# Attention, softplus-tanh layer and experts on one core: weight decoding one piece per step, softmax division moved to VectorE, loads interleaved with the attention steps

## The chip, the cores and the metric

One core of one Trainium2 chip runs the whole program. The time is device microseconds of one execution, and versions are compared by the median of several executions. Engine names below: PE is TensorE, ACT is ScalarE, DVE is VectorE, POOL is GpSimd, and SP is the engine whose queue issues all transfers here.

## What is computed

Three stages follow one another. The first is an attention with two branches for 2 batches, 8 heads, 576 positions and 64 dimensions: a global branch over averages of four positions, and a local branch in which each position sees only the positions less than four away. The second is a dense layer pair, the third eight experts with a balanced gate.

```python
q_d, k_d, v_d = (t.reshape(B, H, S // 4, 4, D).mean(axis=3) for t in (q, k, v))
out_up = np.repeat(sm_attn(q_d, k_d, v_d), 4, axis=2)            # global branch
mask = np.abs(pos[:, None] - pos[None, :]) < 4
scores = np.where(mask, scale * q @ k.T, -1e9)                   # local branch
attn = np.exp(scores - scores.max(-1)); attn = attn / (attn.sum(-1) + 1e-9)
x = (out_up + attn @ v)                                          # 1152 tokens x 512
h = x @ w_in                                                     # 512 -> 2048
g = h * np.tanh(softplus(h))
x = g @ w_out                                                    # 2048 -> 512
out = sum over 8 experts of P[:, e] * (relu(x @ w1[e]) @ w2[e])  # P: gate, balanced in 8 rounds
```

The drawn weights `w_in` and `w_out` arrive as 64-bit floating point numbers; the chip computes on 32-bit ones.

## The kernel before, in words

Products are made from pairs of a rounded part and a rest (`hi` and `lo`), three products for each, so that a 128x128 block of weights meets 288 tokens in three matrix products.

**The start** brings the first half of batch 0's attention alone (the first 54 us, in which the change moves nothing). **The slots** come behind it: the loop `for s in range(NS + LAG)` runs the dense pair as 64 slots. Slot `s` does `gemm1(s)` (12 products of `w_in` into a bank, L505), then `mish(s)` (the elementwise chain L485 to L493, over ACT, POOL and DVE, which ends in `ghi` on ACT and `glo`), and `gemm2(s - 4)` (12 products of `w_out`, L528). A token group has 288 tokens, three attention tiles of 96; slots 0 to 5 work on the first group, 6 to 11 on the second, 12 to 17 on the third.

**The waves** lie in the same slots: while slots 0 to 5 run, the attention of the next three tiles is made, and so on: three waves of six slots, each for half a batch. A wave's steps (`attn_steps`) are called one by one by `pump`, between the matrix products of the slots. A step is one part of a unit. A global unit (`gunit`) and a local unit (`lunit`) have three each: `sc` (scores on PE, maximum on DVE L301, exponentials on ACT L303, row sums and their reciprocals on DVE L305 and L306, multiplication by the reciprocals L308), `tr` (transposes on PE) and `av` (product with the values, sum of both branches L393, `xhi` on ACT L394, `xlo` on DVE L395). Each wave has two global and three local units. The first `gemm1` of the next slot group reads `xhi` and `xlo` of all three tiles. `prep` (L267, L280, L282) turns keys and queries before a wave's units; `prep_v` adds up the values on POOL.

**The decoding** turns the 64-bit weights into 32-bit ones. The 8 column blocks of `w_in` and 8 row blocks of `w_out` form a list of 16 (`ring`), each done as two halves by `w_raw`: one ACT copy (L180), three DVE operations on 128x512 (L181, L183, L184), then the request for the half that comes two halves later (`load_w64`, two buffers `raw64`, 512 KB each). `w_split` cuts a decoded block into `hi` (ACT L190) and `lo` (POOL L191). In each slot the loop calls `w_raw` up to twice: once if the next half is wanted within 16 slots, and again if it is wanted within 6. Blocks 0 and 1 are decoded in the start.

**Order.** Each engine executes its instructions in a fixed order. That order is set when the program is built, by a scheduler that places instructions by its own timeline and may move them ahead of earlier ones; `tc.issue_after(x)` keeps what follows it from being placed ahead of `x`. On the chip an instruction that waits holds up everything behind it on its engine.

**Transfers** of keys, queries and values of the second batch, and of the near rows' values for each tile (`load_vw`, 102 rows), go through SP's one queue. In the before version a wave's steps are: all `prep`, then (in the first wave) the second batch's keys and queries, then the values of three tiles, then the units.

**The experts** come behind slot 63; nothing there is changed.

Of the kernel before, what the change touches and what calls it, by code (L numbers as in the profile page):

```python
# [24 lines left out]
AHEAD = 16  # L25
VWB = 3
# [12 lines left out]
def attn_moe_moe_kernel(  # L39
# [13 lines left out]
    PE, ACT, DVE, POOL, SP = nc.tensor, nc.scalar, nc.vector, nc.gpsimd, nc.sync  # L53
    B, H, S, D = q.shape
# [27 lines left out]
    def f32(a):  # L82
        return a.bitcast(F32)

    def new(pool, shape, dt, tag, bufs=2):
        return pool.tile(shape, dt, tag=tag, name=tag, bufs=bufs)
# [27 lines left out]
    state = {"start": True, "n": 0, "g": 0, "pg": 0}  # L114
# [4 lines left out]
    def at_bank():  # L119
        state["n"] += 1  # L120
        return bank("acc" if state["start"] and state["n"] % 2 else "w")

    last = {}
# [10 lines left out]
    ATT_END = 2 * next(i for i, x in enumerate(items) if x[0] == 3)  # L134
# [12 lines left out]
    need = {(kind, m): 2 * loads[m][0] + LAG * (kind == 2) for m in range(len(order)) for kind in (1, 2)}  # L147
    ring = sorted(need, key=need.get)
    raw64, wraw, whl = {}, {}, {}
    place = {"load": 0, "raw": 0, "split": 0}  # L150
# [15 lines left out]
    def w_raw():  # L166

        n, i = divmod(place["raw"], 2)  # L170
        if n >= len(ring) or n >= place["split"] + RAWB:
            return
        place["raw"] += 1
        if i == 0:
            own = n % RAWB == ERAW
            wraw[n] = new(ap if own else wp, [128, 1024], F32, "rawx" if own else "raw", 1 if own else ERAW)
        w = raw64.pop((n, i)).rearrange("p (n t) -> p n t", t=2)
        c = slice(512 * i, 512 * i + 512)
        lo, hi, x = w[:, :, 0], w[:, :, 1], wraw[n].bitcast(U32)[:, c]
        ACT.activation(out=f32(x), in_=f32(hi), func=AF.Copy, scale=F64_BIAS)  # L180
        DVE.tensor_scalar(out=x, in0=x, scalar1=3, scalar2=0x7FFFFFF8, op0=ALU.logical_shift_left,  # L181
                          op1=ALU.bitwise_and)
        DVE.scalar_tensor_tensor(out=x, in0=hi, scalar=0x80000000, in1=x, op0=ALU.bitwise_and, op1=ALU.bitwise_or)  # L183
        DVE.scalar_tensor_tensor(out=x, in0=lo, scalar=29, in1=x, op0=ALU.logical_shift_right, op1=ALU.bitwise_or)  # L184
        load_w64()
# [109 lines left out]
    def softmax(s3, p, rows, tag):  # L295

        n, nh, nk = s3[0].shape
        den = new(at, [n, 2, nh], F32, tag + "d", 2)
        for par in range(2):
            nm = new(at, [n, nh], F32, tag + "m", 4)  # L300
            DVE.tensor_reduce(out=nm, in_=s3[par], axis=AX.X, op=ALU.max, negate=True)  # L301
            for i in range(nh):
                exps.append(ACT.activation(out=p[par][:, i], in_=s3[par][:, i], func=AF.Exp, bias=nm[:, i:i + 1],  # L303
                                           scale=1.0, accum_out=den[:, par, i:i + 1]))
        DVE.tensor_scalar(out=den, in0=den, scalar1=1e-9, scalar2=rows, op0=ALU.add, op1=ALU.mult)  # L305
        DVE.reciprocal(out=den, in_=den)  # L306
        for par in range(2):
            (DVE if par and state["start"] else POOL).tensor_tensor(  # L308
                out=p[par], in0=p[par], in1=den[:, par].unsqueeze(2).to_broadcast([n, nh, nk]), op=ALU.mult)

    def gunit(b, half, q4):


        u = {}
        hps = (2 * q4, 2 * q4 + 1)

        def sc():
            bks = [at_bank() for _ in range(2)]
            for i, hp in enumerate(hps):
                for par, bk in enumerate(bks):  # L320
                    o = slice(64 * par, 64 * par + 64)
                    PE.matmul(out=bk[:SH, SD * i:SD * i + SD], lhsT=qd[b, half][o, hp, :], rhs=kd[b][o, hp, :],
                              start=True, stop=True)
            for par in range(2):
                u[par] = pg[state["pg"] % PBG]
                state["pg"] += 1
            softmax([bk[:SH, 0:2 * SD].rearrange("p (a b) -> p a b", b=SD) for bk in bks], u, 4.0, "g")

        def tr():
            u["pt"] = new(at, [W, 8 * TQ], F32, "pt", 2)[:SH, 0:8 * SH].rearrange("p (a b) -> p a b", a=8)  # L330
            for par in range(2):
                bk = at_bank()
                for i in range(2):
                    for c in range(2):
                        j = 2 * i + c
                        PE.transpose(out=bk[:SH, SH * j:SH * j + SH], in_=u[par][:, i, SH * c:SH * c + SH],
                                     identity=ident[:SH, :SH])
                ACT.activation(out=u["pt"][:, 4 * par:4 * par + 4, :].rearrange("p a b -> p (a b)"),
                               in_=bk[:SH, 0:4 * SH], func=AF.Copy)

        def av():
            if (b, half) not in odT:
                odT[b, half] = new(at, [128, HP, SH], F32, "odT", 1)
            bk = at_bank()
            for i, hp in enumerate(hps):
                for c in range(2):
                    for par in range(2):
                        PE.matmul(out=bk[64 * par:64 * par + 64, SH * i:SH * i + SH], lhsT=vd[b, c][:, 2 * hp + par, :],
                                  rhs=u["pt"][:, 4 * par + 2 * i + c, :], start=(c == 0), stop=(c == 1))
            ACT.activation(out=odT[b, half][:, hps[0]:hps[0] + 2, :].rearrange("p a b -> p (a b)"),  # L350
                           in_=bk[:, 0:2 * SH], func=AF.Copy)
        return [sc, tr, av]
# [45 lines left out]
    def piped(units):  # L398

        return [units[i - 2 * s][s] for i in range(len(units) + 4) for s in (2, 1, 0) if 0 <= i - 2 * s < len(units)]  # L400

    def hb_steps(hb):

        b, half = divmod(hb, 2)
        st = []
        if half == 0:
            st += [partial(prep, "k", b, 0, hp) for hp in range(HP)]
            st += [partial(prep, "q", b, 0, hp) for hp in range(HP)]
            st += [partial(load4, "v", b, 0), partial(load4, "v", b, 1)]
            st += [partial(prep, "k", b, 1, hp) for hp in range(HP)]  # L410
            st += [partial(load4, "q", b, 1)]
            st += [partial(prep_v, b, 0), partial(prep_v, b, 1)]
        else:
            st += [partial(prep, "q", b, 1, hp) for hp in range(HP)]
            if b + 1 < B:
                st += [partial(load4, "k", b + 1, 0), partial(load4, "q", b + 1, 0), partial(load4, "k", b + 1, 1)]
        return st

    def attn_steps(t0, t1):
        st, units = [], []  # L420
        for t in range(t0, t1):
            if t % 3 == 0:
                st += piped(units) if units else []
                st += hb_steps(t // 3)
                units = [gunit(*divmod(t // 3, 2), i) for i in range(2)]
            if t >= VWB:
                st.append(partial(load_vw, t))
            units.append(lunit(t))
        return st + piped(units)


    groups = [(sum(TPG[:i]), n) for i, n in enumerate(TPG)]
# [159 lines left out]
    for s in range(NS + LAG):  # L592
        if s == NS - 4:
            with tc.issue_after(last["mish"].ins):
                gate()
        for a, b, st in waves:
            if s == b:
                while steps:
                    steps.pop(0)()
            if s == b == waves[-1][1]:  # L600
                at_ctx.close()
                tp = ctx.enter_context(tc.tile_pool(name="tp", bufs=1, side="right", reuse_waits="tile"))
                tx["hi"], tx["lo"] = (tp.tile([128, 3 * KH, NB], F32R, name=f"t{z}") for z in ("hi", "lo"))
            if s == a:
                steps += st
                pump.n, pump.done, pump.at, pump.over = len(steps), 0, 24 * a, FRAC * 24 * (b - a)
        for i in range(2):
            n = place["raw"] // 2
            if n < len(ring) and s >= need[ring[n]] - (6 if i else AHEAD):
                w_raw()  # L610
        n = place["split"]
        if n < len(ring) and 2 * n + 2 <= place["raw"] and free_at(n) <= s:
            w_split()
        if s < NS:
            gemm1(s)
        if s >= LAG:
            gemm2(s - LAG)
# [269 lines left out]
```

## Time and profile before

| what | value |
|---|---|
| median of 3 executions | 1144.62 us (1142.21 to 1146.84) |
| the profiled execution | 1142.54 us |
| its span, first to last instruction | 1140.5 us |
| PE busy in the span | 1093.3 us (96%) |
| DVE, ACT, POOL busy | 624.7, 524.8, 447.6 us |
| mean granted clock of PE | 0.982 of full speed |

The span is 2.04 us shorter than the execution's time. A busy PE is a PE that has a product under way, not one at full rate: the granted clock has to be read beside it. [...]

### The profile page before, as it was taken

Reading aid. Unit: us, or ns where it says so; the run is one execution under the profiler, and the core shown is the slowest. Engines: PE = TensorE matmul, PEld = TensorE weight load, DVE = VectorE, ACT = ScalarE, POOL = GpSimd, SP = SyncE. Lnnn points to the kernel's source line nnn. Section 1 sums busy time; section 2 is a strip of 40 time slices with the busy share of each in tenths; the row PEclk is TensorE's granted clock in tenths of the full one; section 3 lists DMA queues with packets and bytes.
Section 4 is the critical chain, followed back from the end, with each engine's and each line's share of the span. In section 5 each row is a group of like instructions: output and inputs, shape, how many; then the busy total and the mean of one; then the engine's idle time right before and its main releaser. Section 6 shows DMA issues by size and latency. Waiting matters only on the chain.

```text
span 1140.5 us, 19187 instructions
## 1 busy us (share of the span) xinstructions
PE 1093.3 (96%) x7298; PEld 993.1 (87%) x7298; DVE 624.7 (55%) x1332; ACT 524.8 (46%) x1465; POOL 447.6 (39%) x487
## 2 busy tenths in 40 slices
PE   9787899889999999999999999999999999999998
PEld 8766788789999888889988899989998899988997
DVE  5777744797678764444544435444354443544443
ACT  4665677666666734244342443423434244242430
POOL 3564735563744704462240522405325043150400
PEclk9887899999999999999999999999999999999999
DMA  7284510140100210120111201112011120111102
GB/s 182 80 194 126 144 23 1 45 134 9 39 19 19 76 37 31 45 74 19 57 38 37 74 20 56 37 38 75 19 57 37 38 74 26 50 38 38 37 1 83
DMA packets 60199, 63.51 MB, mean 56 GB/s; under 512 B 24204, under 2 KB 44620, under 8 KB 60108
## 3 DMA queue, kind: packets, MB, share of 16 engines
q1 hardware_dynamic: 60108, 62.30, 18.7%
q8 instruction: 57, 0.93, 0.3%
q14 instruction: 34, 0.28, 0.1%
HBM read 59.93 MB, written 2.36 MB: 55 GB/s over the span
## 4 chain that ended last, share of the span: by engine, by line
PE 81%; DVE 5%; POOL 4%; DMA 3%; ACT 3%; issue 2%; SPq 2%; POOLq 0%; ACTq 0%; DVEq 0%
PE w L816 35%; PE acc L778 26%; PE w L505 6%; PE acc L528 6%; PE w L778 4%; PE w L369 1%; DMA raw<-in_moe_w_in_dram 1%; SPq L139 1%; POOL me L486 1%; POOL lo L191 1%; DMA raw<-in_moe_w_out_dram 1%; PE acc L445 1%; POOL vd L291 1%; DMA raw<-in_v_dram 1%; POOL vd L292 1%
## 5 line engine op out<-in xcount | busy, mean ns | idle before, releaser
L816 PE MATMUL w<-wc,hhi 128*128 128x512 f32 x1152 | 362.9, 394 | 0.0
L816 PEld LDWEIGHTS w<-wc,hhi 128*128 128x128 f32 x1152 | 211.2, 189 | 38.0
L816 PE MATMUL w<-wc,hlo 128*128 128x512 f32 x576 | 225.7, 392 | 0.0
L690 POOL TENSOR_TENSOR wc<-raw,wc 128x512 fp32r<-128x512 f32 x64 | 81.8, 1300 | 355.6 <-ACT wc L689 355.2
L778 PE MATMUL acc<-xhi,wb 128*128 128x288 f32 x768 | 168.8, 297 | 2.5 <-DVE xlo L556 2.0
L778 PE MATMUL acc<-thi,wb 128*128 128x288 f32 x768 | 168.7, 295 | 0.0
L827 DVE SCALAR_TENSOR_TENSOR yacc<-w,P,yacc 128x512 f32<-128x512 f32 x126 | 94.3, 749 | 81.1 <-PE w L816 81.1
L778 PEld LDWEIGHTS acc<-xhi,wb 128*128 128x128 f32 x768 | 129.1, 189 | 4.2 <-DVE xlo L556 2.3
L778 PEld LDWEIGHTS acc<-thi,wb 128*128 128x128 f32 x768 | 128.4, 188 | 3.1
L816 PEld LDWEIGHTS w<-wc,hlo 128*128 128x128 f32 x576 | 108.4, 188 | 24.0
L769 ACT ACTIVATE hhi<-acc 128x288 fp32r<-128x288 f32 x128 | 52.2, 410 | 144.6 <-PE acc L778 118.0
L765 ACT ACTIVATE p<-acc 128x288 f32<-128x288 f32 x128 | 52.2, 410 | 142.0 <-PE acc L778 138.3
L778 PE MATMUL acc<-xlo,wb 128*128 128x288 f32 x384 | 114.0, 297 | 0.0
L778 PE MATMUL acc<-tlo,wb 128*128 128x288 f32 x384 | 113.1, 295 | 0.0
L678 POOL TENSOR_TENSOR wb<-raw,wb 128x256 fp32r<-128x256 f32 x96 | 72.4, 756 | 94.2 <-PE acc L778 55.3
L770 DVE SCALAR_TENSOR_TENSOR hlo<-acc,hhi 128x288 fp32r<-128x288 f32 x128 | 58.2, 455 | 78.5 <-ACT hhi L769 76.4
L486 POOL TENSOR_SCALAR me<-me 128x288 f32<-128x288 f32 x64 | 63.1, 986 | 91.4 <-ACT me L485 81.9
L678 POOL TENSOR_TENSOR wb<-sums,wb 128x256 fp32r<-128x256 f32 x128 | 93.4, 748 | 13.6 <-ACT wb L677 12.1
L505 PE MATMUL w<-xhi,hi 128*128 128x288 f32 x256 | 80.5, 316 | 9.6 <-ACT xhi L394 6.3
L791 DVE TENSOR_TENSOR acc<-acc,u 128x288 f32<-128x288 f32 x64 | 29.7, 464 | 90.3 <-PE acc L778 90.0
L505 PE MATMUL w<-xlo,hi 128*128 128x288 f32 x256 | 78.1, 305 | 0.6 <-DVE xlo L395 0.6
L505 PE MATMUL w<-xhi,lo 128*128 128x288 f32 x256 | 77.5, 303 | 0.0
(193 smaller groups left out, 2185.9 us busy)
## 6 DMA issues: line engine op xcount, KB each, us to landing
raw<-in_moe_w_dram SPq DMA_DIRECT2D x64, 512.0 KB
raw<-in_moe_w_in_dram SPq DMA_DIRECT2D x16, 512.0 KB
raw<-in_moe_w_out_dram SPq DMA_DIRECT2D x16, 512.0 KB
vw<-in_v_dram SPq DMA_DIRECT2D x12, 192.0 KB
raw<-in_v_dram SPq DMA_DIRECT2D x8, 288.0 KB
raw<-in_q_dram SPq DMA_DIRECT2D x12, 144.0 KB
out_dram<-yacc SPq DMA_DIRECT2D x6, 256.0 KB
raw<-in_k_dram SPq DMA_DIRECT2D x2, 576.0 KB
```

The lines of the kernel that those rows point to most:

```text
L486: POOL.tensor_scalar(out=e, in0=e, scalar1=EXP20, scalar2=None, op0=ALU.min)
L505: PE.matmul(out=bk, lhsT=a[:, kk, o], rhs=b[:, kk, c0:c0 + n], start=(i == 0), stop=(i == 3 * KD - 1))
L528: PE.matmul(out=bk, lhsT=a[:, h, o], rhs=b, start=(first and i == 0), stop=(end and i == 2))
L678: POOL.tensor_tensor(out=t[:, 1], in0=src[u][w], in1=f32(t[:, 0]), op=ALU.subtract)
L690: POOL.tensor_tensor(out=t[:, 1], in0=r[:, a], in1=f32(t[:, 0]), op=ALU.subtract)
L765: ACT.activation(out=t, in_=bk[u, b], func=AF.Copy)
L769: ACT.activation(out=hi, in_=y, func=AF.Relu)
L770: DVE.scalar_tensor_tensor(out=lo, in0=y, scalar=0.0, in1=f32(hi), op0=ALU.max, op1=ALU.subtract)
L778: PE.matmul(out=bk[u, b], lhsT=wb[2 * h + u, w][:, wz, kk, :], rhs=ops[xz][:, k + kk, o + c:o + c + NP], start=(m < 3 and i == 0), stop=(i ...
L791: DVE.tensor_tensor(out=bk[u, "C"], in0=bk[u, "C"], in1=kept[u, "u2"], op=ALU.add)
L816: PE.matmul(out=bk, lhsT=a[:, f, 128 * j:128 * j + 128], rhs=w[:, b, :], start=(i == 0), stop=(i == 3 * FH - 1))
L827: DVE.scalar_tensor_tensor(out=y, in0=bk, scalar=p, in1=y, op0=ALU.mult, op1=ALU.add)
```

## The change

Three edits, none of which changes what is computed. In the waves both multiplications by the reciprocals (L308) run on DVE, where POOL ran both; in the start DVE and POOL keep one each. The loop calls `w_raw` once in a slot instead of up to twice (twice only in slot 0), after slot 17 only in every second slot unless the half is wanted within four slots, and each call is held behind the last instruction of the slot before's `mish` (the ACT copy that makes `ghi`). The loads of a wave are no longer put in a block ahead of the units: one stands ahead of every second step of the units, the near rows' values first, then the second batch's keys and queries.

```diff
@@ softmax
-            (DVE if par and state["start"] else POOL).tensor_tensor(
+            (DVE if par or not state["start"] else POOL).tensor_tensor(
                 out=p[par], in0=p[par], in1=den[:, par].unsqueeze(2).to_broadcast([n, nh, nk]), op=ALU.mult)
@@ hb_steps
             st += [partial(prep, "q", b, 1, hp) for hp in range(HP)]
-            if b + 1 < B:
-                st += [partial(load4, "k", b + 1, 0), partial(load4, "q", b + 1, 0), partial(load4, "k", b + 1, 1)]
@@ attn_steps
-        st, units = [], []
-        for t in range(t0, t1):
-            if t % 3 == 0:
-                st += piped(units) if units else []
-                st += hb_steps(t // 3)
-                units = [gunit(*divmod(t // 3, 2), i) for i in range(2)]
-            if t >= VWB:
-                st.append(partial(load_vw, t))
-            units.append(lunit(t))
-        return st + piped(units)
+        b, half = divmod(t0 // 3, 2)
+        st, loads_ = hb_steps(t0 // 3), [partial(load_vw, t) for t in range(t0, t1)]
+        if half and b + 1 < B:
+            loads_ += [partial(load4, *x) for x in (("k", b + 1, 0), ("q", b + 1, 0), ("k", b + 1, 1))]
+        units = [gunit(b, half, i) for i in range(2)] + [lunit(t) for t in range(t0, t1)]
+        for i, fn in enumerate(piped(units)):
+            st += ([loads_.pop(0)] if loads_ and i % 2 == 0 else []) + [fn]
+        return st + loads_
@@ the loop over slots
-        for i in range(2):
-            n = place["raw"] // 2
-            if n < len(ring) and s >= need[ring[n]] - (6 if i else AHEAD):
+        n = place["raw"] // 2
+        if n < len(ring) and s >= need[ring[n]] - AHEAD and (s < ATT_END or s % 2 == 0 or s >= need[ring[n]] - 4):
+            if s:
+                with tc.issue_after(last["mish"].ins):
+                    w_raw()
+            else:
+                w_raw()
                 w_raw()
```

How this moves instructions shows on two engines. The first place is ACT at the end of the first wave, before: `ghi` is the last of a slot's `mish`, `pt` are copies of transposed softmax tiles, `raw` and `rawx` are decoded weights, `xhi` the attention's result.

```order
L492 ACTIVATE ghi_1385<-me_1382 128x288
L381 ACTIVATE pt_1369<-w_1376 102x384
L180 ACTIVATE raw_1665<-raw64_1079 128x512
L394 ACTIVATE xhi_107<-w_1404 128x4x96
L180 ACTIVATE rawx_1915<-raw64_1149 128x512
L381 ACTIVATE pt_1423<-w_1424 102x384
L381 ACTIVATE pt_1423<-w_1430 102x384
L180 ACTIVATE rawx_1915<-raw64_1155 128x512
L394 ACTIVATE xhi_107<-w_1441 128x4x96
L180 ACTIVATE raw_2135<-raw64_1670 128x512
L485 ACTIVATE me_1474<-w_1437 128x288
L394 ACTIVATE xhi_107<-w_1458 128x4x96
```

The same place of the changed kernel (its `mish` lines have numbers three lower):

```order
L381 ACTIVATE pt_1404<-w_1405 102x384
L394 ACTIVATE xhi_107<-w_1385 128x4x96
L381 ACTIVATE pt_1404<-w_1411 102x384
L489 ACTIVATE ghi_1366<-me_1363 128x288
L180 ACTIVATE raw_1418<-raw64_996 128x512
L482 ACTIVATE me_1462<-w_1425 128x288
L394 ACTIVATE xhi_107<-w_1429 128x4x96
L190 ACTIVATE hi2_1494<-raw_1418 128x512
L485 ACTIVATE ml_1464<-mm_1463,two_78 128x288
L394 ACTIVATE xhi_107<-w_1446 128x4x96
```

Four decoding copies stood among the three `xhi`; now one does, right behind a `ghi`, and the halves that stood there come one slot each later.

The second place is DVE behind the last wave, in slots 18 to 21, before (`mm`, `w` and `glo` are the `mish` chains of several slots):

```order
L487 SCALAR_TENSOR_TENSOR mm_2791<-me_2790 128x288
L181 TENSOR_SCALAR raw_2816<-raw_2816 128x512 x2
L489 TENSOR_TENSOR w_2777<-mm_2791,w_2777 128x288
L183 SCALAR_TENSOR_TENSOR raw_2816<-raw64_2140,raw_2816 128x512
L183 SCALAR_TENSOR_TENSOR raw_2816<-raw64_2215,raw_2816 128x512
L184 SCALAR_TENSOR_TENSOR raw_2816<-raw64_2140,raw_2816 128x512
L184 SCALAR_TENSOR_TENSOR raw_2816<-raw64_2215,raw_2816 128x512
L491 TENSOR_TENSOR w_2732<-w_2732,ml_2747 128x288
```

And in the changed kernel:

```order
L484 SCALAR_TENSOR_TENSOR mm_2791<-me_2790 128x288
L486 TENSOR_TENSOR w_2777<-mm_2791,w_2777 128x288
L488 TENSOR_TENSOR w_2732<-w_2732,ml_2747 128x288
L488 TENSOR_TENSOR w_2777<-w_2777,ml_2792 128x288
L490 TENSOR_TENSOR glo_2749<-w_2732,ghi_2748 128x288
L490 TENSOR_TENSOR glo_2794<-w_2777,ghi_2793 128x288
```

Both halves of a block stood between the multiplications L489 and L491; they have moved to slots 22 and 24.

The third place is DVE in the third wave, at the second local unit of the changed kernel (`lm` and `ld` are maxima and sums, `pl` the softmax tiles):

```order
L301 TENSOR_REDUCE lm_2423<-w_2410 96x4
L181 TENSOR_SCALAR raw_2298<-raw_2298 128x512
L301 TENSOR_REDUCE lm_2429<-w_2411 96x4
L183 SCALAR_TENSOR_TENSOR raw_2298<-raw64_2057,raw_2298 128x512
L484 SCALAR_TENSOR_TENSOR mm_2461<-me_2460 128x288
L184 SCALAR_TENSOR_TENSOR raw_2298<-raw64_2057,raw_2298 128x512
L486 TENSOR_TENSOR me_2460<-mm_2461,w_2407 128x288
L305 TENSOR_SCALAR ld_2422<-ld_2422 96x8
L306 RECIPROCAL ld_2422<-ld_2422 96x8
L308 TENSOR_TENSOR pl2_96<-pl2_96,ld_2422 96x408
L308 TENSOR_TENSOR pl3_97<-pl3_97,ld_2422 96x408
L301 TENSOR_REDUCE lm_2512<-w_2499 96x4
```

Before, neither the decoding of that half nor the two multiplications stood here; the former was done by the second wave, the latter on POOL.

## Rows read from the trace of the kernel before

**Rows 1.** Stretches: length, PE, PEld, DVE, ACT, POOL busy; clock; DMA share; GB/s.

```profile
54.50:112.90 58.40, 45.01 (x339) 37.41 (x338) 41.33 (x78) 36.32 (x122) 29.67 (x28) 0.86 0.65 155
112.90:163.30 50.40, 44.86 (x383) 39.25 (x383) 32.36 (x71) 34.56 (x125) 30.46 (x35) 0.93 0.35 97
163.30:202.60 39.30, 38.33 (x353) 33.74 (x354) 19.75 (x49) 28.70 (x112) 19.66 (x23) 1.00 0.03 6
202.60:262.00 59.40, 50.87 (x360) 48.95 (x359) 50.38 (x97) 38.68 (x92) 35.13 (x29) 0.97 0.28 90
262.00:300.00 38.00, 38.00 (x289) 38.00 (x288) 24.05 (x58) 22.99 (x55) 15.17 (x15) 1.00 0.04 15
```

**Rows 2.** PE's waits, 56 to 214 us: total, times, longest.

```profile
PE w L505 <- ACT xhi L394: 6.3, 3, 4.6
PE acc L528 <- ACT ghi L492: 4.4, 3, 1.8
PE w L267 <- DMA raw<-in_q_dram: 2.8, 1, 2.8
```

**Rows 3.** ACT in order of time, end of wave one; wait and releaser in brackets.

```profile
108.47 0.66 ACT L180 ACTIVATE rawx<-raw 128x512 f32<-128x512 f32 x1 [1.94 <-DMA raw<-in_moe_w_in_dram]
...
111.53 0.66 ACT L180 ACTIVATE raw<-raw 128x512 f32<-128x512 f32 x1 [2.02 <-DMA raw<-in_moe_w_out_dram]
...
112.38 0.48 ACT L394 ACTIVATE xhi<-w 128x384 fp32r<-128x384 f32 x1
```

**Rows 4.** PE in order of time, the same place.

```profile
112.92 0.61 PE L505 MATMUL w<-xhi,hi 128*128 128x288 f32 x1 [4.60 <-ACT xhi L394]
```

**Rows 5.** Two stretches with a low granted clock; columns as in rows 1.

```profile
82.00:93.00 11.00, 10.88 (x61) 9.27 (x62) 4.12 (x11) 6.67 (x31) 5.24 (x7) 0.53 0.22 71
...
110.00:117.00 7.00, 4.08 (x22) 4.07 (x23) 5.96 (x13) 3.46 (x8) 0.93 (x1) 0.53 0.70 177
```

**Rows 6.** Decoding by stretch (L184 alone, one for each half), waves one, two, slots from 18.

```profile
54.50:112.90 58.40, 10.15 (x11) 0.86 0.65 155
112.90:163.30 50.40, 3.43 (x4) 0.93 0.35 97
...
202.60:262.00 59.40, 9.43 (x12) 0.97 0.28 90
```

**Rows 7.** DVE by line and shape, 0 to 420 us: busy, mean ns, idle before.

```profile
L183 DVE SCALAR_TENSOR_TENSOR raw<-raw,raw 128x512 uint32<-128x512 uint32 x24 | 21.0, 877 | 0.2
...
L184 DVE SCALAR_TENSOR_TENSOR raw<-raw,raw 128x512 uint32<-128x512 uint32 x24 | 20.3, 847 | 0.1
L181 DVE TENSOR_SCALAR raw<-raw 128x512 uint32<-128x512 uint32 x24 | 15.8, 662 | 3.8 <-ACT raw L180 3.7
...
L308 DVE TENSOR_TENSOR pl<-pl,ld 96x408 f32<-96x408 f32 x3 | 2.0, 679 | 0.1
```

**Rows 8.** POOL by line and shape, 0 to 420 us.

```profile
L308 POOL TENSOR_TENSOR pl<-pl,ld 96x408 f32<-96x408 f32 x21 | 20.6, 997 | 16.2 <-DVE ld L306 12.1 <-ACT pt L381 3.5 <-ACT pt L338 0.4
...
L308 POOL TENSOR_TENSOR pg<-pg,gd 72x288 f32<-72x288 f32 x14 | 11.0, 802 | 4.5 <-DVE gd L306 3.0 <-ACT ml L488 0.8 <-PE w L369 0.7
```

**Rows 9.** DVE in order of time: two of the same operation.

```profile
99.19 1.64 DVE L184 SCALAR_TENSOR_TENSOR raw<-raw,raw 128x512 uint32<-128x512 uint32 x1
...
107.00 0.69 DVE L184 SCALAR_TENSOR_TENSOR rawx<-raw,rawx 128x512 uint32<-128x512 uint32 x1
```

**Rows 10.** POOL in order of time, beside the first of them.

```profile
98.74 1.54 POOL L191 TENSOR_TENSOR lo<-raw,hi 128x512 fp32r<-128x512 f32 x1 [2.41 <-ACT hi L190]
```

**Rows 11.** DVE in order of time, slots 18 to 20.

```profile
212.10 2.95 DVE L181 TENSOR_SCALAR raw<-raw 128x512 uint32<-128x512 uint32 x2
...
215.34 1.54 DVE L183 SCALAR_TENSOR_TENSOR raw<-raw,raw 128x512 uint32<-128x512 uint32 x2
216.80 1.28 DVE L184 SCALAR_TENSOR_TENSOR raw<-raw,raw 128x512 uint32<-128x512 uint32 x2
```

**Rows 12.** PE's waits, 202 to 262 us.

```profile
PE acc L528 <- ACT ghi L492: 5.1, 2, 4.3
```

## The prediction

> **What bounds the kernel now.** I first cut the span into stretches and read PE's busy time and its granted clock for each [rows 1]. From 262 us on PE is busy all the time at full clock: there the products themselves are the bound, and the change can at best do no harm. Ahead of that the time is not PE's. In the first wave (58.4 us) PE is idle for 58.4 - 45.0 = 13.4 us and its mean clock is 0.86; with two levels, 1 and 0.5, that is half clock for 28% of the stretch, which costs 0.14 x 58.4 = 8.2 us of work. The second wave loses 5.5 us idle and 0.07 x 50.4 = 3.5 us to the clock, the third 1.0 us in all, and the slots from 18 on 8.5 us idle and 0.03 x 59.4 = 1.8 us. Together that is 41.9 us. No edit can win more than this, and every claim below has to say which part of it goes.
>
> Then I asked whom PE waits for. In the waves it is ACT: 6.3 us for `xhi` and 4.4 us for `ghi`, and 2.8 us for the first query load [rows 2]. The longest wait, 4.6 us, is the one ahead of slot 6's first product [rows 4]. ACT's own order of time says why `xhi` is late [rows 3]: two decoding copies stand ahead of it, and each waits about 2 us for its weights to arrive. ACT can't pass them. Behind that gap the clock is at its lower level for nearly seven microseconds [rows 5]. In the slots from 18 on PE waits 5.1 us for `ghi`, 4.3 us at a time [rows 12], and DVE's order shows what stands ahead of the multiplication that `ghi` needs: six decoding operations in one row, from 212.1 to 218.1 us [rows 11]. So the same work, the decoding, is what PE waits for at both places: 11 halves pass through the first wave, 4 through the second, and 12 through the 59 us from slot 18 on [rows 6].
>
> **The change part by part.**
>
> *Pacing the decoding.* No instruction goes away; the halves move. By the code and the order the first wave keeps 5 of its halves, the second gets 5 or 6, the third 3 or 4, and the last 12 are spread over slots 22 to 46. Between two halves now lies at least one slot, which in the waves is 50.4 / 6 = 8.4 us, against waits of 2 us that are left of each transfer today [rows 3]; so I cost the transfers at nothing, with the slot's own products and softmax as cover. If the cover failed, each half would again hold ACT for about 2 us. What goes in the waves: the 4.6 us for `xhi` [rows 4]; the clock behind it, (1 - 0.53) x 7 = 3.3 us [rows 5]; the 4.4 us for `ghi`, whose chain now runs without decoding in between [rows 2]; and of the other slow stretch, 0.47 x 11 = 5.2 us [rows 5], I take half, since I can't tell from the trace what brought it on. Sum 14.9 us. It could be as little as the 4.6 us alone, if other waits move up behind the rest; and with all of the slow stretch, both clocks and the other waits for `xhi`, 19 us. The 2.8 us for the query load stays: its request stands where it stood.
>
> *The slots from 18 on.* With the halves at slots 22, 24, 26 and 28 instead of 18 to 21, the block of six operations ahead of `ghi` is gone. The loss there is 10.3 us [rows 1]; I take 7, the 5.1 us of [rows 12] and the clock's 1.8. Bounds 2 and 10: the splits (ACT L190, POOL L191) stay where they were and keep POOL busy.
>
> *What this hands on.* The eight halves that run today before 262 us come to lie in slots 32 to 46, where DVE has 24.1 of 38 us busy [rows 1]. A half costs DVE 0.66 + 0.88 + 0.85 = 2.4 us by the means [rows 7]; the operations overlap a little at their ends, so I take 2. Six or seven of them fall in this stretch: 24 + 13 = 37 of 38 us. DVE is then as full as PE. The chain has four slots of slack, so I put 2 us on it, with 0 and 8 as bounds (8: 13 us of decoding more, of which only the 14 - 8 = 6 idle ones would cover).
>
> *The multiplications.* Thirty L308 leave POOL, where they take 1.0 us (local) and 0.8 us (global) [rows 8], and come to DVE, at 0.68 us [rows 7]: 30 x 0.68 = 20.4 us more on DVE. They stand in the chain of a unit in both versions, so each pair gets 2 x 0.3 = 0.6 us shorter for a local unit if DVE is free. It is not always free: behind L305, which waits for the exponentials, everything queues, the `mish` operations of the next slot too, and they make `glo` and `ghi` late next. In the first wave DVE goes from 41.3 us to 41.3 - 5 x 2 + 6.8 = 38, so it is relieved. In the second it goes from 32.4 to 32.4 + 3 + 6.8 = 42 of 50, in the third from 19.8 to 19.8 + 7 + 6.8 = 34 of 39 us [rows 1]. The third wave had nothing to lose, so what is added there costs. I take 5 us for the two waves together. Lower bound 0 (the cover is PE's own products, 38 us in the third wave), upper bound all twenty multiplications on the path, 13.6 us.
>
> POOL and DVE also disturb each other: the same L184 takes 0.69 us alone and 1.64 us [rows 9] while POOL runs a subtraction of 1.54 us [rows 10]. [...] By rows alone, if every one of the thirty took 0.95 us longer, DVE would have 28 us more to do; at the share of the added work that I put on the path, 5 of 20, that is 7 us, and the sum below would be half as large. Against it: the same edit takes 31.6 us of work away from POOL [rows 8], which is then busy half as long and meets DVE less often. I leave it out of the sum and among the rivals.
>
> *The loads.* Six requests for near rows now stand ahead of the twelve for keys and queries on SP's queue. None of the waits of [rows 2] is for one of these, before the change; keys and queries are wanted only in the second wave, tens of microseconds later. Price 0, with the first wave's units as cover. Without cover one such load costs what the first query load costs, 2.8 us.
>
> *Sum.* -14.9 - 7 + 2 + 5 = -14.9 us, say -15. The profiled execution took 1142.54 us, which gives 1127.5. The median of the three runs is 1144.62, 2.1 above it, so I forecast **1130 us** for the median.
>
> **The rivals.**
>
> *DVE takes the waits over (about no change).* The decoding's waits go, but DVE, at 42 of 50 and 34 of 39 us in waves two and three and 37 of 38 behind, holds up `ghi` and `glo` instead. Gains of 4.6 + 7 us against 8 + 5: 1144.6 + 1 = 1146, and with half of the gain 1140. For it: the numbers of the parts just worked out, and L184's mean of 0.85 us [rows 7] against 0.69 alone [rows 9]. Against it: DVE was 85% busy from 202 to 262 us and PE still busy 86% [rows 1]; the share alone does not stop PE.
>
> *DVE and POOL hold each other up.* If all thirty multiplications take as much longer as the slower L184 of [rows 9], the 7 us worked out above go from the gain: 1137. For it: that pair of rows; against it: POOL has 31.6 us less to do. [...]
>
> *All of it goes.* The slow clock follows the gaps; without them it does not fall. Then 31 us of the 41.9 go: 1114. For it: the third wave runs at full clock with 1 us idle; against it: it had neither decoding nor loads nor, on DVE, multiplications.
>
> *Slower.* In waves two and three each local unit's multiplications wait behind L305 on DVE for its exponentials, with two `mish` operations behind them. If each of the 10 units of these waves makes PE wait 3 us, that is 30 us against gains of at most 22: 1152. It decides from 2.2 us a unit on. For it: DVE waits for ACT there already; against it: the scheduler has put other work between L305 and the scores, and before the change PE hardly waits for a softmax tile.
>
> *The change does nothing.* Not possible for the order, which shows the moves; for the time only if other waits stood right behind, which is the first rival.
>
> **How the numbers follow.** A measurement can tell about 0.5%, 5.7 us, from no change, so faster means under 1138.9. The forecast, 1120 to 1137, gets 0.58; all of it, 1106 to 1119, 0.12; DVE and POOL in each other's way, about 1137, 0.06; DVE takes over, 1139 to 1150, 0.16; slower 0.08. That makes 0.76 faster, 0.16 same, 0.08 slower. The range from 1112 to 1144 leaves out about 0.06 below and 0.13 above. If the likeliest case holds, 1119 to 1137.
>
> **What would show it.** In the first wave's end no decoding copy on ACT should wait for a transfer, and slot 6 should start without the 4.6 us; the first wave should take 46 to 50 us instead of 58, the third 40 to 44. Its clock should be above 0.9. From slot 18 on `ghi` should not wait for L181 to L184, and the stretch to slot 32 should lose under 4 us. DVE should be 85 to 95% busy in slots 32 to 46 with PE above 95%. Wrong would be: PE waiting for `pl` or `pg` from DVE for 10 us or more, a clock at 0.5 for as long as before behind new gaps, or waits for `glo` in slots 32 to 46.

## The result and the profile after

The changed kernel takes **1126.52 us** (median of four executions, 1121.73 to 1129.15), the kernel before 1144.52 us beside it: ratio 0.9832, 95% interval 0.9804 to 0.986. That is faster by 18 us, and 3.5 us below the forecast. The profiled execution is the slowest of the four, 1129.15 us (span 1127.4), so it stands 2.6 us above its median, where that of before (1142.54 us) stood 2.0 below. A profile shows one execution; I use it for places and causes, and medians for sums.

The stretches of the changed kernel, cut at the first product of slots 0, 6, 12, 18, 32 and 48 (columns as in [rows 1]):

```profile
54.46:101.55 47.09, 38.57 (x336) 32.70 (x335) 35.60 (x74) 32.87 (x117) 18.40 (x17) 0.96 0.62 134
101.55:160.48 58.93, 53.51 (x401) 46.76 (x400) 39.13 (x85) 36.49 (x129) 26.85 (x27) 0.80 0.35 95
160.48:196.49 36.01, 35.09 (x340) 31.60 (x339) 28.80 (x67) 28.38 (x112) 10.41 (x11) 1.00 0.21 62
196.49:238.58 42.09, 41.10 (x302) 39.98 (x301) 31.14 (x66) 31.06 (x75) 31.20 (x27) 1.00 0.17 51
238.58:289.90 51.32, 51.32 (x389) 51.32 (x388) 40.95 (x92) 33.34 (x79) 22.86 (x23) 1.00 0.26 83
```

The kernel before, whose first two stretches stand in [rows 1], with the same cuts for the last three:

```profile
163.28:202.14 38.86, 37.89 (x351) 33.30 (x351) 19.31 (x49) 28.44 (x112) 19.55 (x22) 1.00 0.03 6
202.14:254.23 52.09, 43.56 (x302) 41.64 (x303) 43.20 (x79) 32.77 (x78) 33.16 (x27) 0.97 0.29 92
254.23:304.89 50.66, 50.66 (x384) 50.66 (x383) 34.92 (x81) 30.62 (x74) 21.89 (x22) 1.00 0.10 32
```

Read each row for two losses: length less PE busy (idle), and one less the clock, times the length (half clock). Cut into half microseconds (before from 80 to 120 us, changed from 118 to 158), the granted clock is 1.00 or 0.50, and between them only where it changes. Slots 18 to 32 lost 8.5 us idle and lose 1.0; they are 10.0 us shorter. The first wave is 11.3 us shorter. The second is 8.6 us longer, mostly because its clock is 0.80: 11.8 us of half clock, against 3.5 before. The third looks 2.9 us shorter, but its idle time is the same (1.0 and 0.9): it holds fewer products, which the order placed ahead of its first one (351 and 340). Lengths of neighbouring stretches are therefore not compared one by one below; losses are.

PE's waits in the three waves of the changed kernel, which answer to [rows 2]:

```profile
PE acc L525 <- POOL glo L490: 3.2, 3, 2.1
PE w L267 <- DMA raw<-in_q_dram: 2.6, 1, 2.6
PE w L322 <- ACT pg L303: 1.4, 2, 0.9
PE w L336 <- DVE pg L308: 1.3, 1, 1.3
PE w L387 <- ACT pl L303: 1.1, 1, 1.1
PE w L336 <- DVE gd L305: 1.0, 1, 1.0
PE w L380 <- ACT pl L303: 1.0, 1, 1.0
PE acc L525 <- ACT ghi L489: 0.9, 1, 0.9
```

`xhi` is gone from the list, `ghi` fell from 4.4 to 0.9, and in their place come waits of about 1 us for softmax tiles and 3.2 us for `glo`. ACT's order at the end of the first wave, which answers to [rows 3], shows why `xhi` is in time:

```profile
96.17 0.45 ACT L489 ACTIVATE ghi<-me 128x288 fp32r<-128x288 f32 x1 [0.25 <-DVE me L488]
96.52 0.65 ACT L180 ACTIVATE raw<-raw 128x512 f32<-128x512 f32 x1
97.07 0.40 ACT L482 ACTIVATE me<-w 128x288 f32<-128x288 f32 x1
99.12 0.49 ACT L394 ACTIVATE xhi<-w 128x384 fp32r<-128x384 f32 x1 [1.65 <-DVE w L393]
```

The decoding copy L180 stands right behind a `ghi` and waits for nothing: its weights have landed.

### The profile page after: what moved, and what is told of

It reads as the page before. It is cut to its first block, busy times and chain, and to the rows that moved or that the text cites. A ratio compares the mean times of both kernels' runs of the same rounds, so it can differ in the third digit from the quotient of the medians.

```text
span 1127.4 us, 19164 instructions
## 1 busy us (share of the span) xinstructions
PE 1089.8 (97%) x7298; PEld 992.1 (88%) x7298; DVE 632.8 (56%) x1362; ACT 524.0 (46%) x1465; POOL 423.2 (38%) x457
## 3 DMA queue, kind: packets, MB, share of 16 engines
q1 hardware_dynamic: 60108, 62.30, 18.8%
## 4 chain that ended last, share of the span: by engine, by line
PE 84%; DVE 6%; ACT 3%; POOL 3%; issue 1%; DMA 1%; SPq 1%; DVEq 0%; ACTq 0%; POOLq 0%
PE w L817 35%; PE acc L779 25%; PE w L502 7%; PE acc L525 6%; PE w L779 4%; PE w L369 1%; ACT pl L303 1%; PE acc L442 1%; SPq L139 1%; DVE mm L484 1%; POOL vd L291 1%; DMA raw<-in_v_dram 1%; POOL vd L293 1%; DVE sums L673 0%; PE w L387 0%
## 5 line engine op out<-in xcount | busy, mean ns | idle before, releaser
L770 ACT ACTIVATE hhi<-acc 128x288 fp32r<-128x288 f32 x128 | 52.2, 409 | 143.8 <-PE acc L779 118.1
L766 ACT ACTIVATE p<-acc 128x288 f32<-128x288 f32 x128 | 52.1, 409 | 142.2 <-PE acc L779 138.4
L525 PE MATMUL acc<-glo,hi 128*128 128x288 f32 x256 | 74.4, 300 | 3.3 <-POOL glo L490 3.2
```

What stands on the lines that cost most here:

```text
L525: PE.matmul(out=bk, lhsT=a[:, h, o], rhs=b, start=(first and i == 0), stop=(end and i == 2))
L766: ACT.activation(out=t, in_=bk[u, b], func=AF.Copy)
L770: ACT.activation(out=hi, in_=y, func=AF.Relu)
```

## The experiments

Each experiment had six or twelve executions beside the kernel before, and has one profile. "Losses" are worked out as above, from rows like those shown. "Waves" is slots 0 to 18 together.

| version | median us | profiled us | waves: idle, half clock | slots 18 to 32: length, idle |
|---|---|---|---|---|
| before | 1144.5 | 1142.5 | 19.9, 11.7 | 52.1, 8.5 |
| changed | 1126.5 | 1129.2 | 14.9, 13.7 | 42.1, 1.0 |
| e1 pacing alone | 1137.4 | 1139.0 | 19.8, 15.6 | 42.1, 0.9 |
| e2 no pacing | 1155.6 | 1155.1 | 18.6, 30.9 | 51.9, 7.1 |
| e3 division alone | 1146.0 | 1145.5 | 15.4, 10.2 | 55.1, 8.9 |
| e4 no loads' edit | 1141.3 | 1141.1 | 16.7, 18.9 | 42.1, 1.0 |
| e5 holding alone | 1133.6 | 1142.1 | 18.8, 22.0 | 43.0, 1.6 |
| e6 one call a slot alone | 1147.2 | 1145.8 | 18.4, 13.6 | 52.2, 8.3 |
| e7 no division | 1138.4 | 1141.0 | 18.2, 18.6 | 42.2, 0.9 |
| e8 additions on DVE | 1128.4 | 1130.2 | 15.7, 11.9 | 42.1, 1.0 |
| e9 held, up to two calls | 1133.4 | 1133.5 | 15.4, 20.5 | 43.0, 1.7 |
| e10 block, empty steps | 1124.8 | 1120.0 | 14.6, 7.0 | 42.2, 0.9 |
| e11 query earlier | 1123.0 | 1118.4 | 10.7, 5.0 | 42.1, 1.0 |
| e12 loads alone | 1147.5 | 1145.8 | 21.1, 13.2 | 53.5, 8.1 |

**The edits alone, and all but one.** Of the diff, the loop over slots is the pacing, `softmax` the division, `hb_steps` and `attn_steps` together the loads. e1 is the kernel before with the pacing alone, e3 with the division alone, e12 with the loads alone; e2, e4 and e7 are the changed kernel without the pacing, the loads and the division. Of these edits only e7's is shown; the others are the same pieces of the diff.

```diff
@@ e7, softmax of the changed kernel
-            (DVE if par or not state["start"] else POOL).tensor_tensor(
+            (DVE if par and state["start"] else POOL).tensor_tensor(
```

Of e1 was expected:

> The kernel before with the paced decoding alone (multiplications on POOL and the loads in a block, as before). Theory pacing: the decoding's place carries the gain; slot 6 starts by 104 us instead of 113, the slots 18 to 32 take 43 us instead of 52, the median lies at 1124 to 1132. Rival division: the relief of POOL carries it; then this run stays at 1138 to 1145.

Of e2 was expected:

> The changed kernel with the decoding called as before, up to twice a slot and held behind nothing. Theory pacing: the waits for xhi and ghi come back, slots 18 to 32 take 50 us or more, median 1138 to 1150 (DVE has the multiplications on top). Rival division: 1124 to 1132.

Of e3 was expected:

> The kernel before with the multiplications on DVE alone. Theory pacing: no gain, 1141 to 1152, since DVE gets 20 us of work where the decoding already crowds it. Rival division: 1125 to 1135, with the waits for the softmax tiles gone.

Of e4 was expected:

> The changed kernel with the loads in a block ahead of the units, as before. Theory: the transfers are covered either way, the median is within 0.5% of the changed kernel, 1121 to 1132. Rival loads: near rows' values queued behind keys and queries hold up the first wave, 1133 or more, with waits for the values in the first wave.

Of e7 was expected:

> The changed kernel with the multiplications on POOL again: pacing and spread loads alone. If the edits' prices added up (division 0 by its run alone, loads 15 by the run without them), it takes 1122 to 1130. Theory that the edits need each other, because a wait of 2 us for a softmax tile from POOL brings the low clock whatever else is gone: PE waits 2 us and more at a time for pl and pg from POOL, the first two waves together lose over 10 us to the clock, and the time is 1133 to 1142.

Of e12 was expected:

> The kernel before with the loads' edit alone: requests between the units' steps. If the spacing that it makes has a price of its own, 15 us by the run without it, 1127 to 1133. Theory that it is worth something only where neither the decoding nor a multiplication on POOL holds up a unit's softmax (by the runs of pacing with loads and of division with loads): the slots from 18 to 32 stay at 52 us, the waves at 145 us or more, and the time is 1142 to 1156.

Measured: e1 0.9928 (0.9901 to 0.9954), half of what was expected; e2 1.0081 (1.0051 to 1.011), slower than before; e3 1.0013 (0.9993 to 1.0034); e4 0.9953 (0.9932 to 0.9974), where I had expected the loads to be worth nothing; e7 0.9945 (0.992 to 0.997); e12 1.0006 (0.9982 to 1.0031). e2's waits came back as expected (2.3 us for `xhi` and 2.6 for `ghi` in the waves, 51.9 us in slots 18 to 32), but its time lies above the range that I gave it. In microseconds by these ratios (times 1144.5), pacing alone is worth -8, division +1.5 and loads +0.7 (these two within their noise), -6 together; all three give -19. Taken out of the finished kernel they cost 28 (pacing), 13 (division) and 14 us (loads). The prices don't add up; prices of single edits, which is how I made my sum, are not a property of the edit.

Where division without pacing can hurt shows in e2, which is 9 us slower than the loads alone (e12). DVE in order of time, from a unit's maximum L301 to its multiplication L308:

```profile
97.03 0.57 DVE L301 TENSOR_REDUCE lm<-w 96x4 f32<-96x408 f32 x1
97.52 0.67 DVE L183 SCALAR_TENSOR_TENSOR raw<-raw,raw 128x512 uint32<-128x512 uint32 x1
98.12 1.52 DVE L484 SCALAR_TENSOR_TENSOR mm<-me 128x288 f32<-128x288 f32 x1
99.57 0.68 DVE L184 SCALAR_TENSOR_TENSOR raw<-raw,raw 128x512 uint32<-128x512 uint32 x1
...
101.42 1.07 DVE L308 TENSOR_TENSOR pl<-pl,ld 96x408 f32<-96x408 f32 x2
```

and PE behind it:

```profile
102.15 1.17 PE L380 MATMUL w<-ident,pl 96*102 96x96 f32 x6 [2.89 <-DVE pl L308]
```

Two decoding operations stand in the unit's chain on DVE, and PE waits 2.89 us for `pl`. How much of the wait is theirs isn't separated: L484 between them took 1.52 us, where its median in the changed kernel's waves is 0.45, and most of e2's loss is half clock, 30.9 us in the waves against 11.7 before. In the opposite case, pacing with the division left on POOL, PE waits for POOL (e1, waits in the waves):

```profile
PE w L336 <- POOL pg L308: 5.1, 3, 2.5
PE w L380 <- POOL pl L308: 3.0, 2, 2.3
```

**Which half of the pacing.** e5 keeps up to two calls a slot but holds them behind `mish`; e6 lowers the number and doesn't hold; e9 is the changed kernel with e5's loop.

```diff
@@ e5, the loop of the kernel before
             if n < len(ring) and s >= need[ring[n]] - (6 if i else AHEAD):
-                w_raw()
+                if s:
+                    with tc.issue_after(last["mish"].ins):
+                        w_raw()
+                else:
+                    w_raw()
```

Of e5 was expected:

> The kernel before, where each call of the decoding is held behind the slot's mish, but still up to two calls a slot as before. Theory that the number of halves per slot is what counts: slots 18 to 32 keep their length of 52 us and their wait for ghi of about 4 us, and the time is 1140 to 1149. Rival, that it is the holding behind mish: slots 18 to 32 take 42 us as with the whole pacing, and the time is 1132 to 1138.

Of e6 was expected:

> The kernel before, with one decoding call a slot (every second slot after slot 17), not held. Theory that the number per slot counts: slots 18 to 32 take 42 to 43 us, 10 less than before, and the time is 1130 to 1139. Rival, that the holding counts: they take 48 to 53 us and the time is 1140 to 1149.

Of e9 was expected:

> The changed kernel with the pacing's holding behind mish, but up to two decoding calls a slot as before. Theory that the holding is the pacing's working part and that the lower number per slot is worth nothing (by the runs of either half alone): 1118 to 1129, slots 18 to 32 take 42 to 44 us. Rival, that in the waves the lower number is wanted as well: waits of 2 us on ACT for the weights come back at the end of the first wave, PE waits 2 us or more for xhi at slot 6, and the time is 1130 to 1140.

Measured: e5 0.9904 (0.9871 to 0.9937), e6 1.002 (1.0 to 1.0041), e9 0.9902 (0.9876 to 0.9927). My first theory fell: the lower number alone does nothing. DVE of e6 in slots 18 to 20 shows the same row as [rows 11]; the scheduler still pulls two halves together:

```profile
214.74 2.95 DVE L181 TENSOR_SCALAR raw<-raw 128x512 uint32<-128x512 uint32 x2
217.61 0.45 DVE L489 TENSOR_TENSOR w<-mm,w 128x288 f32<-128x288 f32 x1
217.97 1.54 DVE L183 SCALAR_TENSOR_TENSOR raw<-raw,raw 128x512 uint32<-128x512 uint32 x2
219.44 1.28 DVE L184 SCALAR_TENSOR_TENSOR raw<-raw,raw 128x512 uint32<-128x512 uint32 x2
```

and PE's first row behind them waits 4.31 us:

```profile
221.59 0.80 PE L528 MATMUL acc<-ghi,hi 128*128 128x288 f32 x4 [4.31 <-ACT ghi L492]
```

With the holding, slots 18 to 32 take 42.1 to 43.0 us in all nine versions that have it; in the five without they take 51.9 to 55.1. That is settled. In e9 the lower number is missing and the kernel is 7 us slower than the changed one, so in company of the other edits it is worth something; its profile has no 2 us wait for `xhi`, which the rival wanted, but 20.5 us of half clock in the waves.

**What the loads' edit does.** e10 requests all of a wave's loads in one step and leaves empty steps between the units' steps.

```diff
-        for i, fn in enumerate(piped(units)):
-            st += ([loads_.pop(0)] if loads_ and i % 2 == 0 else []) + [fn]
-        return st + loads_
+        st.append(lambda: [fn() for fn in loads_])
+        for i, fn in enumerate(piped(units)):
+            st += ([lambda: None] if i < 2 * len(loads_) and i % 2 == 0 else []) + [fn]
+        return st
```

Of e10 was expected:

> The changed kernel with all loads of a wave requested in one step ahead of the units, and an empty step where each load stood. Theory that the loads' worth is the room that a step without a product makes between two steps of the units, so that a unit's softmax has longer: as the changed kernel, 1122 to 1131. Rival, that it is the order of the requests (near rows first, keys and queries later): as without the edit, 1135 to 1144.

Measured 1124.76 us, 0.9835 (0.9805 to 0.9864): as the changed kernel. So the 14 us are not for spreading the requests in time: what e4 lacks is the place of the units' steps among the slots' products. (e10 still asks for the near rows first, so it doesn't test that order. But in e4's waves PE's only wait for a transfer is the first query load's, 2.8 us against 2.6 in the changed kernel.) In e4 the first local unit's multiplications start at 89.42 us, 33.8 us behind the first product of slot 0; in the changed kernel it is 26.1 us (80.52), in e10 29.1. The second unit's, closer behind in e4, meet POOL. The two engines of e4:

```profile
93.48 3.22 DVE L308 TENSOR_TENSOR pl<-pl,ld 96x408 f32<-96x408 f32 x2
```

```profile
93.15 3.11 POOL L191 TENSOR_TENSOR lo<-raw,hi 128x512 fp32r<-128x512 f32 x2
```

The changed kernel's DVE at its third local unit, and POOL, which has been idle for 3.90 us when its next operation starts:

```profile
93.19 1.07 DVE L308 TENSOR_TENSOR pl<-pl,ld 96x408 f32<-96x408 f32 x2
```

```profile
94.52 1.29 POOL L191 TENSOR_TENSOR lo<-raw,hi 128x512 fp32r<-128x512 f32 x1 [3.90 <-ACT hi L190]
```

Beside POOL's subtractions the two multiplications took 3.22 us instead of 1.07. What that costs PE is not shown: the product behind the slow pair, at 97.12 us, shows no wait. e4's waves have 1.8 us more idle time (its waits for `pg` from DVE come to 2.9 us, in the changed kernel to 1.3) and 5.2 us more half clock, 18.9 against 13.7.

**The wait for `glo`.** In the changed kernel's second wave half clock follows a wait for `glo`, which stands on POOL behind the values' additions (L293 at 118.23 us for 2.02 and L292 at 120.22 for 0.71, then `glo` at 120.90). e8 makes these additions one reduction on DVE for each piece.

```diff
             a, z = x[:, 4 * i:4 * i + 4], src[:, 4 * i:4 * i + 4]
+            if not state["start"]:
+                DVE.tensor_reduce(out=a, in_=z.rearrange("s h r d -> s h d r"), axis=AX.X, op=ALU.add)
+                continue
             POOL.tensor_tensor(out=a, in0=z[:, :, 0, :], in1=z[:, :, 1, :], op=ALU.add)
```

Of e8 was expected:

> The changed kernel, in which the additions of the values (three on POOL for each of 4 pieces, 12 us together) are one reduction each on DVE. Theory that the changed kernel's second wave is slow because glo stands on POOL behind these additions, PE then waits 2.1 us for it and the low clock of 122 to 156 us follows: the wait for glo and most of that stretch go, the second wave takes 46 to 50 us instead of 58.9, and the time is 1112 to 1120. Rival, that the low clock comes there whatever PE waits for, or that DVE then makes PE wait instead: 1123 to 1132.

Measured 1128.37 us, 0.9847 (0.9819 to 0.9875): no gain, and my theory failed. The wait for `glo` is gone (0.2 us left), but others came (PE's longest in e8's waves):

```profile
PE w L267 <- DMA raw<-in_q_dram: 2.8, 1, 2.8
PE w L267 <- DVE me L489: 2.1, 1, 2.1
PE w L339 <- DVE pg L311: 2.0, 2, 1.3
```

and half clock moved to the first wave (0.86 in 55.38:105.52). e10 has a gap at the same place, a little shorter. The changed kernel, the product behind the gap:

```profile
122.20 0.40 PE L525 MATMUL acc<-glo,hi 128*128 128x288 f32 x1 [2.13 <-POOL glo L490]
```

and the 20 us that follow:

```profile
122.00:142.00 20.00, 19.80 (x108) 16.85 (x109) 12.59 (x28) 12.09 (x53) 8.36 (x8) 0.57 0.17 56
```

The same two of e10:

```profile
122.81 0.40 PE L526 MATMUL acc<-glo,hi 128*128 128x288 f32 x1 [1.88 <-POOL glo L491]
```

```profile
122.00:142.00 20.00, 18.08 (x163) 15.06 (x164) 16.45 (x37) 15.44 (x68) 8.38 (x10) 1.00 0.24 80
```

Once 108 products at a clock of 0.57, once 163 at 1.00. The two are not quite alike: in the changed kernel PE had waited another 0.47 us at 118.65, for `pg`. A closer pair stands in the last section.

**The query load.** e11 requests the first wave's query load in the start, ahead of the weight loads on SP's queue (in the changed kernel two of `w_in` stand there from 51.79 to 55.39 us, the query load's requests from 55.44). The definition of `next_q`, which makes the same four requests, is left out here.

```diff
-        return st + [g[1], h[1], g[2], a[1], h[2], c[1], a[2], e[1], c[2], e[2]]
+        return st + [g[1], h[1], g[2], a[1], next_q, h[2], c[1], a[2], e[1], c[2], e[2]]
...
-    waves = [(6 * i, 6 * i + 6, [partial(load4, "q", 0, 1)] * (i == 0) + attn_steps(3 * i + 3, 3 * i + 6)) for i in range(3)]
+    waves = [(6 * i, 6 * i + 6, attn_steps(3 * i + 3, 3 * i + 6)) for i in range(3)]
```

Of e11 was expected:

> The changed kernel, whose first query load (batch 0, second half) is requested in the start instead of behind a 512 KB weight load. Theory that PE's 2.6 us wait for it and the low clock that follows such waits are a loss of their own: the wait goes, the first wave takes 43 to 46 us, and the time is 1117 to 1124. Rival, that the next wait moves up behind it: 1125 to 1131.

Measured 1122.98 us, 0.9814 (0.9785 to 0.9844), within what the first theory expected. Its first wave:

```profile
54.60:98.33 43.73, 39.41 (x338) 34.90 (x339) 33.85 (x72) 31.05 (x114) 19.04 (x17) 0.92 0.59 140
```

4.3 us idle instead of 8.5. The wait for the query load is gone, but the edit also takes one step out of the first wave, and by e10 steps matter; the two are not told apart. The interval overlaps with the changed kernel's, so that it is faster than that one is likely, not shown; it is the lowest median of all.

## Why the prediction was right, point by point

**Pacing in the waves, -14.9.** The waits went as said: `xhi` 6.3 to 0, `ghi` 4.4 to 0.9, the query load stayed. But the idle time of the waves fell by only 5.0 us (19.9 to 14.9), since waits for `glo`, `pg` and `pl` moved up: 0.7 us of `glo` before became 3.2. The 5.9 us of clock in this term did not come in the profiled execution (11.7 before, 13.7 after). That pair is not typical, though. The span and the mean granted clock of every execution are on record; one less the clock, times the span, is the half clock of the whole execution. Its median is 26.3 us in the 74 executions of the kernel before beside the experiments (20.5 in the profiled one) and 17.4 in the four of the changed kernel (19.2 in the profiled one). 3.3 us of the term were also misread: the window of [rows 5], 110 to 117 us, begins in the gap itself. From the product at 112.92 us on the half clock costs about 1.9 us; PE was idle ahead of it.

And the term belongs to no single edit: e1 gains 7 to 8 us in all, and from slot 18 to the end it is 7.0 us shorter (931.3 us against 938.3 before), so pacing alone is worth about nothing in the waves. The three edits together take 930.9 us from slot 18 on, 7.4 less than before; of the 18 us by the medians, some 10.6 are then left for the waves (5.6 in the profiled executions). I had -14.9 and +5.

**Slots 18 to 32, -7.** Right in mechanism, mis-sized: -10.0, my bound. I took 5.1 us of waits and the clock; the stretch gave back nearly all its idle time and all its half clock. What I called spreading is, by e5 and e6, the holding.

**Handed on, +2.** Right in size and kind, but just behind slots 32 to 48. In slots 32 to 48 PE is busy for all of 51.32 us, with five products more than in the row of before; DVE is busy 40.95 of it, 80%, not 85 to 95. But right behind that cut PE waits 2.8 us in the changed kernel, where before it waits 0.2:

```profile
294.21 0.40 PE L502 MATMUL w<-xhi,hi 128*128 128x288 f32 x1 [0.83 <-DVE glo L490]
299.14 0.80 PE L525 MATMUL acc<-ghi,hi 128*128 128x288 f32 x4 [1.99 <-ACT ghi L489]
```

On DVE the last decoded half stands ahead of the multiplication that this `ghi` needs:

```profile
296.12 1.77 DVE L183 SCALAR_TENSOR_TENSOR rawx<-raw,rawx 128x512 uint32<-128x512 uint32 x1
297.82 0.45 DVE L486 TENSOR_TENSOR w<-mm,w 128x288 f32<-128x288 f32 x1
298.18 0.45 DVE L488 TENSOR_TENSOR w<-w,ml 128x288 f32<-128x288 f32 x1
```

It takes the lower number and the holding together to move this half so far back: e1 has both waits too, while e6 is done with the decoding at 263.8 us and e5 and e9 at 285.9 and 276.6, without them (e5 and e9 have one of 1.0 us for `ysum`). From slot 18 to the end e5 and e9 take 928.5 and 929.4 us.

**The multiplications, +5.** The step that failed: "The third wave had nothing to lose, so what is added there costs." Nothing was lost there (idle 1.0 and 0.9), although DVE went from 19.31 to 28.80 us; busy share said nothing of order. In the finished kernel this edit is worth -13 us (e7), alone nothing (e3).

**The loads, 0.** Right alone (e12), wrong in company: -14 (e4). I costed the transfers and overlooked that a load is also a step, which moves the others (e10).

The sum of -15 came near -18, and so did its two places: -9.9 in the waves against some -10.6, and -5 behind slot 18 against -7.4. In the waves that is in part luck, since the single terms were not: pacing alone brought about nothing there, and the +5 and the 0 of the other two edits were gains once it was in. Of the signs of being wrong that I had named, one came in the profiled execution: a clock near 0.5 for as long as before, behind a new gap, the one for `glo`.

**The rivals.** *DVE takes the waits over* is not what happened to the changed kernel, but for the 2.8 us behind slot 48; where pacing is missing, e2 has one wait of this kind, the 2.89 us for `pl`. *DVE and POOL hold each other up*: in the changed kernel DVE's L184 on `raw` took 0.729 us in the mean instead of 0.847, and its L308 on `pl` 0.636:

```profile
L184 DVE SCALAR_TENSOR_TENSOR raw<-raw,raw 128x512 uint32<-128x512 uint32 x24 | 17.5, 729 | 0.2
L308 DVE TENSOR_TENSOR pl<-pl,ld 96x408 f32<-96x408 f32 x21 | 12.7, 636 | 0.4
```

So it was rightly left out, but e4 has a case of it: a pair of L308 took 3.22 us beside POOL's subtractions, 1.07 in the changed kernel. What spoke against it was too high in the prediction: the 31.6 us of [rows 8] hold five multiplications of the start, which stay on POOL. By the means there the thirty took 27.6 us, and POOL in the waves is busy 55.7 instead of 79.7 us, not half as long. *All of it goes*, for whose 31 us the prediction gives no working, did not: 14.9 us of idle time and 13.7 of half clock are left in the waves. *Slower* was wrong: PE has no wait for a local tile from DVE's L308 in the waves.

**What stays open.** Among the versions with the holding, the five at 1133 to 1141 us (e1, e4, e5, e7, e9) have 15.6 to 22.0 us of half clock in the waves, the four at 1123 to 1128 (changed, e8, e10, e11) 5.0 to 13.7; idle times are 15.4 to 19.8 and 10.7 to 15.7. These are single profiles: e5's was 8.5 us above its median, those of e10 and e11 almost 5 below. Over all executions, with the rest as the span less its half clock (medians, us):

| version | executions | half clock | rest |
|---|---|---|---|
| before | 74 | 26.3 | 1115.8 |
| changed | 4 | 17.4 | 1107.3 |
| e4 no loads' edit | 12 | 29.0 | 1109.4 |
| e7 no division | 12 | 22.7 | 1114.6 |
| e9 held, up to two calls | 6 | 25.5 | 1106.6 |

So about half of the gain is clock. What e4 and e9 lack is nearly all clock; what e7 lacks is in the larger part the rest, where the waits are. What sets the clock I can't say: neither the longest gap nor the sum of the gaps orders the versions. The wave part of the gain is therefore measured as a sum, and not traced to single waits.

## What to carry to other kernels

Hold work with slack behind the critical chain whose in-order engines it shares; calling it less often was not enough here, since the scheduler pulled it forward. Cost edits to one chain together: here three edits were worth -6 us by their single runs and -19 together, and one of them worked through the step that it inserted, not through what the step did. Compare losses (idle, clock) per stretch rather than lengths, since work can cross a cut.

## What the hardware showed unexpectedly

The same gap was followed by half clock in one run and not in another: the 6 us behind it have a clock of 0.50 in e7 and of 1.00 in e6. In e7 and e6 PE waits for the first query load at the same place, for the same time, and was busy for 2.49 and 2.50 us of the 6 us ahead of the product. e7, the product and the 6 us from it on:

```profile
61.00 0.35 PE L267 MATMUL w<-ident,raw 72*128 72x72 f32 x1 [2.91 <-DMA raw<-in_q_dram]
```

```profile
61.00:67.00 6.00, 5.79 (x28) 5.42 (x28) 1.55 (x3) 2.29 (x7) 1.83 (x2) 0.50 1.16 174
```

The same two of e6:

```profile
63.12 0.25 PE L267 MATMUL w<-ident,raw 72*128 72x72 f32 x1 [2.90 <-DMA raw<-in_q_dram]
```

```profile
63.12:69.12 6.00, 5.08 (x39) 4.49 (x40) 5.79 (x11) 4.30 (x11) 4.02 (x4) 1.00 1.02 209
```

What decides between the two no run here shows. Behind e6's 2.90 us the clock stayed at 1.00, so the rival's premise, that the slow clock follows the gaps, does not hold for every gap. The theory put down for e7, that a wait of 2 us for a softmax tile from POOL brings the low clock, is not shown: PE's longest wait for one in e7 is 1.2 us (`pg`).

Executions of one version differ by up to 12 us (e4: 1131.82 to 1143.82), as much as an edit is worth here.
